# Second of seven projection products moved between the seventh and the third, fifth ahead of sixth, in blocks 2 to 5 of an attention and SwiGLU kernel

## The chip, the core and the metric

The kernel runs on one core of a Trainium2 chip. A core has five engines with their own instruction queues: TensorE (PE, matmuls; its weight loads are listed apart as PEld), VectorE (DVE), ScalarE (ACT), GpSimd (POOL) and SyncE (SP). An engine works through its queue in order and waits on semaphores for the others. The metric is the device time of one execution in microseconds (us); the figure for the kernel before is the median of nine runs.

## The reference

Two stages. Attention over 8 batches, 8 heads, 576 positions and head size 64, with a window of 128 positions and a bias that falls linearly with the distance; then a SwiGLU feed-forward over all 8 x 576 = 4608 tokens, model size 512, inner size 1536:

```python
scores = np.where(mask, scale * q @ k.T + bias, -1e9)   # mask: 0 <= i - j < 128
x = softmax(scores) @ v                                 # heads side by side: 4608 x 512
g = x @ w_gate
out = (g / (1 + exp(-g)) * (x @ w_val)) @ w_out         # float32
```

## The kernel before

**Blocks.** The feed-forward takes the tokens in nine blocks of 512 (`n` = 0 to 8). For a block, the gate and value products run over twelve slices `m` of the inner size: four 512-column matmuls into a PSUM tile `pg` for the gate, four into `pv` for the value. This text calls each of these groups of four a half step; a block has 24, numbered 0 to 23 (2 x `m` for the gate, 2 x `m` + 1 for the value). ACT makes `tt`, a tanh of the gate (L415), DVE makes `uu` from `tt` and `pg` (L416), and DVE multiplies `uu` by `pv` into `hT` (L427). `pg` and `pv` rotate through three PSUM banks.

**Attention** runs interleaved with blocks 0 to 5: scores (`ps`, L278, groups of eight matmuls; `psc`, L313), their exp on ACT (`ex`, L284; `exc`, L317), a multiply by decay factors or masks on DVE (L290, L321), weighted sums of values (`av`, L345), a division on DVE (L347, L348 into `x`), and a transpose of `x` on PE (`px`, L371) with an ACT copy, or by DMA on SP's queue. Scores, `av`, `px` and the tile `p2` described below share a pool of four PSUM banks, `ps_a`.

**The output projection by seven products.** The projection of block `n` - 1 is done during block `n`. Its tile of 512 tokens and its 512 output columns are each cut in two, the inner size is cut in two as well, and the 2 x 2 block product is made with seven products in place of eight (Strassen's scheme in Winograd's form). The function is `strassen(n, t)`; `t` is 0 or 1, each covers half of the rows of both token halves, so a block's projection is two runs of seven products, 14 in all. This text calls them the first half and the second half of the products of a block. A product is six 256-column matmuls (L532). Products are numbered as their helper names in the seven-product stage:

- first: `X` = A11 B11; ACT copies it out as `p1s`
- second: `p2` = A12 B21, in its own bank of `ps_a`; DVE adds `p1s` and makes the upper left quarter (profile name `osb<-p,p1s`)
- sixth: `X` += S2 T2; ACT copies it out as `u2s`
- fifth: `Y` = S1 T1; ACT copies it out as `p5s`
- seventh: `X` += S3 T3; DVE adds `p5s`, lower right quarter (`osb<-po,p5s`)
- third: `Y` += S4 B22; DVE adds `u2s`, upper right quarter (`osb<-po,u2s`), and SP stores the 128 rows
- fourth: `X` += A22 T4; ACT copies the lower left quarter out, and SP stores

`X` and `Y` are the two halves of one PSUM bank, the tile `po`, of which there is one. A product that writes there waits until the eviction of the product before it has read the bank. T1 to T4 are sums of parts of `w_out`, made once. S1 to S4 are sums of parts of `hT`, made on DVE by `sums(n, c)` in three thirds, c = 0, 1, 2, with four operations each (L485 to L488: S3, S1 in place of A21, S2, S4). They are queued in the list `later` from slice `m` = 9 on, and one or two are issued after each half step, so that the last third is issued during the first half steps of the next block. Third `c` is read by the matmuls 2c and 2c + 1 of a product's six.

**The order.** PE's order is the order of the program from step 60 on (`FIXED_FROM`), and blocks 2 to 5 lie there. In these blocks `AT` lists the half steps after which one product is issued; attention steps are issued by a count of the steps done so far. DVE's and ACT's order, the assignment of banks and the place of DMA instructions on SP are chosen by a scheduler when the program is built. POOL's queue is written out by hand. Blocks 6 to 8 have another scheme (`seven_steps`), in which gate and value products are also made by seven products; the projections of blocks 5 to 8 run there.

Of the kernel before, what the change touches and what calls it, by code (L numbers as in the profile page):

```python
# [51 lines left out]
def kernel(  # L52
# [10 lines left out]
    nc = tc.nc  # L63
    B, H, S, D = q.shape
    NTOK, DM = out.shape
# [370 lines left out]
    def rows_of(n, j):  # L436
        if n == 8:
            return [(0, 64, 2 * j * S + 512), (64, 128, (2 * j + 1) * S + 512)]
        return [(0, 128, n * S + j * P)]

    def store(n, j, osb, c0=0, c1=512, two=False):
        for i, (p0, p1, r0) in enumerate(rows_of(n, j)):
            (nc.scalar if two and i else nc.sync).dma_start(out[r0:r0 + p1 - p0, c0:c1],
                                                            osb[p0:p1, c0:c1])
# [18 lines left out]
    HC = DM // 2  # L463
    T1, T2, T3, T4 = (consts.tile([P, HM, HC], FP16, name=f"T{n}") for n in (1, 2, 3, 4))
    B11, B12 = wo_sb[:, 0:HM, 0:HC], wo_sb[:, 0:HM, HC:DM]
    B21, B22 = wo_sb[:, HM:NMB, 0:HC], wo_sb[:, HM:NMB, HC:DM]
# [37 lines left out]
    def strassen(n, t):  # L504

        h = hT[n]
        A11, A12 = h[:, 0:HM, 0:256], h[:, HM:NMB, 0:256]
        S1, A22 = h[:, 0:HM, 256:512], h[:, HM:NMB, 256:512]
        S2, S3, S4 = hsum[n]
        cols = slice(t * P, (t + 1) * P)  # L510
        end = n == NBLK - 1
        seeded = SEVEN_FROM <= n + 1 < NBLK
        factor = 1.0 if n >= SEVEN_FROM else 0.5
        if end:
            X, Y = (ps_a.tile([P, HC], FP32, name="po", tag="a", bufs=4) for _ in range(2))
            p2 = ps_f.tile([P, HC], FP32, name="p2", tag="gv")
        else:
            po = ps_f.tile([P, 2, HC], FP32, name="po", tag="po", bufs=1)
            X, Y = po[:, 0, :], po[:, 1, :]
            p2 = (ps_f.tile([P, HC], FP32, name="p2", tag="gv") if seeded  # L520
                  else ps_a.tile([P, HC], FP32, name="p2", tag="a"))
        top, low = (opool.tile([P, DM], FP32, name="osb", tag="osb") for _ in range(2))
        if end and t:
            spare = [opool.tile([P, DM], FP32, name="osb", tag="osb") for _ in range(2)]
            p1s, p5s, u2s = spare[0][:, 0:HC], spare[0][:, HC:DM], spare[1][:, 0:HC]
        else:
            p1s, p5s, u2s = (supool.tile([P, HC], FP32, name=i, tag=i, bufs=1)
                             for i in ("p1s", "p5s", "u2s"))

        def product(dst, a, b, start=False):  # L530
            for m in range(HM):
                nc.tensor.matmul(dst, a[:, m, cols], b[:, m, :], start=(start and m == 0),  # L532
                                 stop=(m == HM - 1), skip_group_check=True)

        def half_plus(dst, a, b):
            nc.vector.scalar_tensor_tensor(out=dst, in0=a, scalar=factor, in1=b,
                                           op0=ALU.mult, op1=ALU.add)

        product(X, A11, B11, True)
        if seeded:  # L540
            nc.scalar.copy(p2, X)
        else:
            nc.scalar.mul(p1s, X, factor)
        yield
        product(p2, A12, B21, not seeded)
        if seeded:
            nc.vector.tensor_scalar_mul(top[:, 0:HC], p2, factor)
        else:
            half_plus(top[:, 0:HC], p2, p1s)
        if end and t:  # L550
            store(n, t, top, 0, HC)
        yield
        product(X, S2, T2)
        nc.scalar.mul(u2s, X, factor)
        yield
        product(Y, S1, T1, end)
        if end and t:
            nc.vector.tensor_scalar_mul(p5s, Y, factor)
        else:
            nc.scalar.mul(p5s, Y, factor)  # L560
        yield
        product(X, S3, T3)
        half_plus(low[:, HC:DM], X, p5s)
        if end and t:
            store(n, t + 2, low, HC, DM, True)
        yield
        product(Y, S4, B22)
        half_plus(top[:, HC:DM], Y, u2s)
        store(n, t, top, HC if end and t else 0, DM, end)
        yield  # L570
        product(X, A22, T4)
        if end:
            nc.vector.tensor_scalar_mul(low[:, 0:HC], X, factor)
        else:
            nc.scalar.mul(low[:, 0:HC], X, factor)
        store(n, t + 2, low, 0, HC if end and t else DM, end)
        yield
# [118 lines left out]
                    of[which[0]][name](which[1])  # L696
                yield n, 7 * u + k, name, which

    AT = {1, 3, 4, 6, 8, 9, 11, 12, 14, 16, 17, 19, 20, 22}

    def ffn():

        for n in range(NBLK):
            if n > 1:
                parts = chain(strassen(n - 1, 0), strassen(n - 1, 1))
# [6 lines left out]
            for m in range(NMB):  # L712
                for half, _ in enumerate(gate_val(n, m)):
                    yield 1.0
                    if n > 1 and 2 * m + half in AT:
                        next(parts)
# [21 lines left out]
            if n > 1:  # L738
                assert next(parts, 0) == 0
        ends = [strassen(NBLK - 1, t) for t in range(2)]  # L740
        final = ()
        for n, k, name, which in seven_steps():
            if k == 0 and n > SEVEN_FROM:
                assert next(parts, 0) == 0
                parts = chain(strassen(n - 1, 0), strassen(n - 1, 1))
            if n == SEVEN_FROM and k in (1, 3, 10, 17):
                later.extend(gate_val_weight_sums(2 + (k + 4) // 7))
            yield 0.5
            if k % 3 == 2 and k < 42:
                next(parts)  # L750
                yield 0.75
            if k == 20 and n + 1 < NBLK:
                later.extend(x_sums(n + 1))
            if k == 35:
                later.extend(sums(n, 0))
            if name == "fourth" and which is not None and which[1] > 3:
                if which == (NBLK - 1, 5):
                    at_once(final)
                else:
                    later.extend(sums(which[0], which[1] - 3))  # L760
            if n == NBLK - 1 and k == 40:
                final = sums(n, 2)
                later.append(final.pop(0))
            for _ in range(2 if len(later) > 4 or k >= 39 or k < 7 else 1):
                if later:
                    later.pop(0)()
            if n == NBLK - 1 and k == 41:
                next(ends[0])
                yield 0.75
# [235 lines left out]
```

## Time and profile before

| | |
|---|---|
| median of nine runs | 345.09 us (344.87 to 345.57) |
| the profiled execution | 345.07 us, of which the span from first to last instruction is 343.3 us |
| PE busy | 329.1 us, 96% of the span |
| DVE busy | 277.6 us, 81% |
| ACT busy | 207.6 us, 60% |
| TensorE clock granted | 0.999 of full speed |
| the chain that ended last | PE 69%, DVE 19%, ACT 4%, DMA 4%, issue 3% of the span |
| first product of blocks 2, 3, 4, 5 starts at | 97.3, 136.2, 174.7, 212.5 us |
| seven-product stage starts at | 245.2 us |

Busy time is the sum of an engine's instruction records. PE's matmuls overlap, so the record of six 256-column matmuls is 0.82 us long while the next group starts 0.65 us after it; for times on PE the distance between starts is the better measure. DVE's and ACT's records overlap a little as well. A wait is put down to the engine and the line that released it.

### The profile page before, as it was taken

Reading aid. Unit: us, or ns where it says so; the run is one execution under the profiler, and the core shown is the slowest. Engines: PE = TensorE matmul, PEld = TensorE weight load, DVE = VectorE, ACT = ScalarE, POOL = GpSimd, SP = SyncE. Lnnn points to the kernel's source line nnn. Section 1 sums busy time; section 2 is a strip of 40 time slices with the busy share of each in tenths; the row PEclk is TensorE's granted clock in tenths of the full one; section 3 lists DMA queues with packets and bytes.
Section 4 is the critical chain, followed back from the end, with each engine's and each line's share of the span. In section 5 each row is a group of like instructions: output and inputs, shape, how many; then the busy total and the mean of one; then the engine's idle time right before and its main releaser. Section 6 shows DMA issues by size and latency. Waiting matters only on the chain.

```text
span 343.3 us, 7778 instructions
## 1 busy us (share of the span) xinstructions
PE 329.1 (96%) x2983; PEld 218.3 (64%) x2983; DVE 277.6 (81%) x652; ACT 207.6 (60%) x412; POOL 109.6 (32%) x136
## 2 busy tenths in 40 slices
PE   7999989999999999999999999999999999999995
PEld 3484455444456565666565655565788878888884
DVE  6578886999798679988899999999855975775683
ACT  3758676565666755756556557563467666676640
POOL 8968672649765076834017000000000000000000
PEclk9999999999999999999999999999999999999999
DMA  9999999999999999999939914021101101011014
GB/s 150 168 180 177 164 175 146 91 147 160 139 172 149 149 178 160 162 165 151 186 107 107 173 32 78 15 73 37 63 2 61 63 0 64 13 51 63 0 71 116
DMA packets 160037, 37.37 MB, mean 109 GB/s; under 512 B 147328, under 2 KB 155648, under 8 KB 160000
## 3 DMA queue, kind: packets, MB, share of 16 engines
q0 software_dynamic: 118336, 18.62, 84.1%
q1 hardware_dynamic: 40976, 17.64, 27.7%
q10 hardware_dynamic: 688, 0.62, 0.6%
q8 instruction: 23, 0.38, 0.5%
q14 instruction: 14, 0.11, 0.1%
HBM read 37.91 MB, written 9.44 MB: 138 GB/s over the span
## 4 chain that ended last, share of the span: by engine, by line
PE 69%; DVE 19%; ACT 4%; DMA 4%; issue 3%; POOL 0%; ACTq 0%; DVEq 0%
PE po L532 15%; PE pv L397 13%; PE pg L397 13%; PE gX L623 8%; PE gY L623 4%; PE av L345 3%; PE ps L278 3%; DVE uu L416 3%; DMA qn<-in_q_dram 3%; DVE hT L427 2%; PE p L532 2%; PE po L451 2%; PE gZ L623 2%; DVE x L348 2%; ACT ex L284 2%
## 5 line engine op out<-in xcount | busy, mean ns | idle before, releaser
L397 PE MATMUL pv<-xT,wv_sb 128*128 128x512 f16 (+2 forms) x320 | 76.5, 358 | 0.4 <-DVE hT L427 0.2
L397 PE MATMUL pg<-xT,wg_sb 128*128 128x512 f16 (+2 forms) x320 | 75.8, 358 | 0.3 <-DVE xT L373 0.2
L415 ACT ACTIVATE tt<-pg 128x512 f16<-128x512 f32 (+2 forms) x70 | 41.3, 590 | 50.4 <-PE pg L397 49.4
L284 ACT ACTIVATE ex<-ps 128x512 f16<-128x512 f32 x96 | 50.0, 606 | 11.3 <-PE ps L278 11.3
L416 DVE SCALAR_TENSOR_TENSOR uu<-tt,pg 128x512 f16<-128x512 f16 (+2 forms) x69 | 46.0, 666 | 10.4 <-ACT tt L415 10.2
L427 DVE TENSOR_TENSOR hT<-uu,pv 128x512 f16<-128x512 f16 (+2 forms) x70 | 46.7, 666 | 3.6 <-PE pv L397 1.6
L185 POOL DMA_DIRECT2D va<-in_v_dram x40 | 34.3, 865 | 38.3 <-PE av L345 31.9
L397 PEld LDWEIGHTS <-wg_sb 128*128 128x128 f16 x320 | 28.3, 98 | 24.1 <-issue 2.3
L532 PEld LDWEIGHTS <-hT 128*128 128x128 f16 x384 | 36.8, 98 | 10.4 <-issue 1.1
L397 PEld LDWEIGHTS <-wv_sb 128*128 128x128 f16 x320 | 28.3, 98 | 23.7 <-issue 2.6
L191 POOL DMA_DIRECT2D kn<-in_k_dram x39 | 33.3, 859 | 18.7 <-DMA kT<-kn 10.1
L191 POOL DMA_DIRECT2D qn<-in_q_dram x39 | 33.4, 863 | 16.1 <-DMA va<-in_v_dram 8.5
L532 PEld LDWEIGHTS <-S 128*128 128x128 f16 x288 | 27.7, 98 | 10.7 <-issue 2.5
L290 DVE TENSOR_TENSOR ex<-ex,m_reg 128x1024 f16<-128x1024 f16 x42 | 28.7, 687 | 3.2 <-ACT ex L284 3.1
L348 DVE TENSOR_TENSOR x<-av,rec 128x256 f16<-128x256 f32 x72 | 28.5, 419 | 0.4
L532 PE MATMUL po<-T,S 128*128 128x256 f16 x192 | 26.5, 273 | 0.5 <-DVE S L487 0.5
L532 PE MATMUL po<-T,hT 128*128 128x256 f16 x192 | 26.1, 273 | 0.0
L317 ACT ACTIVATE exc<-psc 128x512 f16<-128x512 f32 x40 | 21.3, 608 | 4.1 <-PE psc L313 4.1
L675 DVE TENSOR_TENSOR hT<-s,v 128x512 f16<-128x512 f16 x18 | 7.6, 424 | 18.5 <-ACT s L674 18.5
L345 PEld LDWEIGHTS <-ex 128*128 128x128 f16 x384 | 17.4, 97 | 4.6 <-issue 1.1
L345 PE MATMUL av<-va,ex 128*128 128x65 f16 x384 | 19.3, 194 | 0.7 <-ACT ex L284 0.7
L278 PE MATMUL ps<-qT,kT 64*128 64x256 f16 x192 | 16.6, 273 | 0.4 <-DVE qT L223 0.2
(134 smaller groups left out, 535.9 us busy)
## 6 DMA issues: line engine op xcount, KB each, us to landing
out_dram<-osb SPq DMA_DIRECT2D x32, 256.0 KB, 2.5
va<-in_v_dram POOLq DMA_DIRECT2D x32, 128.0 KB, 8.2
qn<-in_q_dram POOLq DMA_DIRECT2D x31, 128.0 KB, 8.7
kn<-in_k_dram POOLq DMA_DIRECT2D x31, 128.0 KB, 9.2
wg_sb<-in_moe_w_gate_dram POOLq DMA_DIRECT2D x6, 256.0 KB, 7.5
wv_sb<-in_moe_w_val_dram POOLq DMA_DIRECT2D x6, 256.0 KB, 8.0
wo_sb<-in_moe_w_out_dram POOLq DMA_DIRECT2D x2, 768.0 KB, 9.5
kn<-in_k_dram POOLq DMA_DIRECT2D x8, 64.0 KB, 7.0
```

The costliest lines, as they stand in the source:

```text
L185: nc.gpsimd.dma_start(va[rank][p0:p1, :, 0:D], src)
L191: nc.gpsimd.dma_start(t_[p0:p1], src)
L284: nc.scalar.activation(e[:, o:o + 2, :], banks[q4][par], AF.Exp, scale=scale)
L290: nc.vector.tensor_mul(e[:, o, :], e[:, o, :], reg[:, o, :])
L345: nc.tensor.matmul(av[:, j, :], w, val, start=(n == 0), stop=(n == len(todo) - 1))
L348: nc.vector.tensor_mul(x[:, 4 * half:4 * half + 4, :], av[:, :, 0:D], rec.broadcast_to([P, 4, D]))
L397: nc.tensor.matmul(ps[:, c0:c1], w[:, kb, ms], xT[n][:, kb, c0:c1], start=(kb == 0 and c0 == 0), stop=(kb == NKB - 1 and c1 == 512), skip_ ...
L415: nc.scalar.activation(tt, pg[:, c0:c1], AF.Tanh, scale=0.5)
L416: nc.vector.scalar_tensor_tensor(out=uu, in0=tt, scalar=one if (n, m) == PIN else 1.0, in1=pg[:, c0:c1], op0=ALU.add, op1=ALU.mult)
L427: nc.vector.tensor_mul(hT[n][:, m, c0:c1], acted[(n, m)][1][:, c0:c1], pv[:, c0:c1])
L532: nc.tensor.matmul(dst, a[:, m, cols], b[:, m, :], start=(start and m == 0), stop=(m == HM - 1), skip_group_check=True)
L623: nc.tensor.matmul(dst[:, i, :], w[:, kb, c0 + i * P:c0 + (i + 1) * P], a[:, kb, :], start=(start and i == 0 and kb == 0), stop=(i == 1 an ...
```

## The change

In `strassen` the steps become small functions, and their order depends on the block. Where the projection is that of blocks 1 to 4 (so in the blocks 2 to 5 of gate and value work) the order first, second, sixth, fifth, seventh, third, fourth becomes first, fifth, sixth, seventh, second, third, fourth. For the projections of blocks 5 to 8 it stays. `AT` gets other half steps for the 14 products:

| | first half of the products | second half |
|---|---|---|
| before | first 1, second 3, sixth 4, fifth 6, seventh 8, third 9, fourth 11 | first 12, second 14, sixth 16, fifth 17, seventh 19, third 20, fourth 22 |
| after | first 1, fifth 3, sixth 5, seventh 7, second 8, third 9, fourth 11 | first 13, fifth 15, sixth 17, seventh 19, second 20, third 21, fourth 23 |

The diff, with the bodies of the small functions left out; they hold the lines of before, unchanged:

```diff
-        product(X, A11, B11, True)
...
-        product(p2, A12, B21, not seeded)
...
-        product(X, S2, T2)
...
-        product(Y, S1, T1, end)
...
-        product(X, S3, T3)
...
-        product(Y, S4, B22)
...
+        def first():
+            product(X, A11, B11, True)
...
+        def second():
+            product(p2, A12, B21, not seeded)
...
+        def sixth():
+            product(X, S2, T2)
+            nc.scalar.mul(u2s, X, factor)
...
+        def fifth():
+            product(Y, S1, T1, end)
...
+        def seventh():
+            product(X, S3, T3)
+            half_plus(low[:, HC:DM], X, p5s)
...
+        def third():
+            product(Y, S4, B22)
+            half_plus(top[:, HC:DM], Y, u2s)
...
+        for step in ((first, second, sixth, fifth, seventh, third) if seeded or end
+                     else (first, fifth, sixth, seventh, second, third)):
+            step()
+            yield
         product(X, A22, T4)
...
-    AT = {1, 3, 4, 6, 8, 9, 11, 12, 14, 16, 17, 19, 20, 22}
+    AT = {1, 3, 5, 7, 8, 9, 11, 13, 15, 17, 19, 20, 21, 23}
```

In the built program PE, DVE, ACT and POOL have the same instructions as before. The order changes on PE, DVE and ACT from block 2 on, two transposes on SP change places with a store each, and POOL's order is the same.

More of the change, by code (lines that the diff above doesn't have):

```diff
@@ L537, in half_plus @@
                                            op0=ALU.mult, op1=ALU.add)
-        product(X, A11, B11, True)
[L540 to L544, printed above, removed]
-        product(p2, A12, B21, not seeded)
[L546 to L552, printed above, removed]
@@ L553, in strassen @@
-        product(X, S2, T2)
-        nc.scalar.mul(u2s, X, factor)
-        yield
-        product(Y, S1, T1, end)
[L557 to L561, printed above, removed]
-        product(X, S3, T3)
[L563 to L566, printed above, removed]
-        product(Y, S4, B22)
-        half_plus(top[:, HC:DM], Y, u2s)
-        store(n, t, top, HC if end and t else 0, DM, end)
@@ L570, in strassen @@
-        yield
+        def first():
+            product(X, A11, B11, True)
+            if seeded:
+                nc.scalar.copy(p2, X)
+            else:
+                nc.scalar.mul(p1s, X, factor)
+        def second():
+            product(p2, A12, B21, not seeded)
+            if seeded:
+                nc.vector.tensor_scalar_mul(top[:, 0:HC], p2, factor)
+            else:
+                half_plus(top[:, 0:HC], p2, p1s)
+            if end and t:
+                store(n, t, top, 0, HC)
@@ new lines, in sixth @@
+        def sixth():
[3 more added lines that the diff above has]
+            product(Y, S1, T1, end)
+            if end and t:
+                nc.vector.tensor_scalar_mul(p5s, Y, factor)
+            else:
+                nc.scalar.mul(p5s, Y, factor)
+        def seventh():
+            product(X, S3, T3)
+            half_plus(low[:, HC:DM], X, p5s)
+            if end and t:
+                store(n, t + 2, low, HC, DM, True)
+        def third():
+            product(Y, S4, B22)
+            half_plus(top[:, HC:DM], Y, u2s)
+            store(n, t, top, HC if end and t else 0, DM, end)
```

## The prediction

> **What bounds the kernel now.** I read the page's busy shares first, then PE's waits in the stretch where blocks 2 to 5 run (95 to 247 us), then four stages, then single places of the timeline. Columns of the page's first part are busy us, share of the span, instructions.
>
> ```profile
> PE 329.1 (96%) x2983; PEld 218.3 (64%) x2983; DVE 277.6 (81%) x652; ACT 207.6 (60%) x412; POOL 109.6 (32%) x136
> ```
>
> PE is the bound, so time can only be won where PE stands still. The waits of PE in the stretch (total, times, longest):
>
> ```profile
> PE po L532 <- DVE osb L536: 1.5, 2, 0.8
> PE p L532 <- ACT ex L284: 0.7, 1, 0.7
> PE av L345 <- ACT ex L284: 0.7, 2, 0.5
> PE po L532 <- DVE S L487: 0.5, 1, 0.5
> PE psc L313 <- DVE osb L536: 0.2, 1, 0.2
> ```
>
> All but the third are in steps that the change moves. The stages (length, then PE, PEld, DVE, ACT, POOL busy, granted clock, DMA):
>
> ```profile
> 95.00:165.00 70.00, 69.08 (x653) 42.22 (x653) 59.69 (x136) 45.41 (x92) 35.12 (x42) 1.00 1.97 161
> 165.00:194.00 29.00, 27.53 (x247) 16.73 (x246) 28.87 (x73) 15.70 (x33) 7.59 (x10) 1.00 1.44 136
> 194.00:245.00 51.00, 50.33 (x435) 30.11 (x434) 49.84 (x123) 26.89 (x53) 0.00 (x0) 1.00 0.24 58
> ```
>
> From 165 to 194 DVE works 28.87 of 29.00 us. There PE does not wait because its products are in a bad order; it waits because DVE is full, and a wait taken away at one place can come back at the next. The places, in PE's and DVE's timeline (start, length, instruction, idle before it):
>
> ```profile
> 118.06 0.61 PE L278 MATMUL ps<-qT,kT 64*128 64x256 f16 x8
> 119.36 0.82 PE L532 MATMUL p<-wo_sb,hT 128*128 128x256 f16 x6 [0.69 <-ACT ex L284]
> 139.23 0.82 PE L532 MATMUL p<-wo_sb,hT 128*128 128x256 f16 x6
> 140.17 0.42 DVE L486 TENSOR_TENSOR hT<-hT 128x512 f16<-128x512 f16 x1
> 166.91 0.39 PE L371 MATMUL px<-idm,x 128*128 128x128 f16 x4
> 167.92 0.81 PE L532 MATMUL po<-wo_sb,S 128*128 128x256 f16 x6 [0.63 <-DVE osb L536]
> 187.26 0.61 PE L278 MATMUL ps<-qT,kT 64*128 64x256 f16 x8
> 188.72 0.82 PE L532 MATMUL po<-wo_sb,S 128*128 128x256 f16 x6 [0.84 <-DVE osb L536]
> 216.90 0.60 PE L532 MATMUL po<-T,S 128*128 128x256 f16 x4
> 218.02 0.39 PE L532 MATMUL po<-T,S 128*128 128x256 f16 x2 [0.52 <-DVE S L487]
> 218.95 0.38 PE L313 MATMUL psc<-qT,kT 64*128 64x128 f16 x7 [0.15 <-DVE osb L536]
> ```
>
> Undisturbed, start to start, a half step (four 512-column matmuls) takes 0.86, a product (six 256-column ones) 0.65, eight score matmuls 0.54, a px 0.22. So the stalls cost: 119.36 (second waits for its bank, still read by an exp) 1.30 - 0.54 = 0.76; 167.92 (third waits for seventh's eviction) 1.01 - 0.22 = 0.79; 188.72 (the same) 1.46 - 0.54 = 0.92; block 5, sixth waits for S2 and the scores after it for second's bank, 1.45 - 0.65 and 0.91 - 0.55 = 1.16. A small one is in front of third at 129.21: the half step there takes 1.06, so 0.20. Together 3.83 us, all that can be won. In DVE's timeline a 512-column operation follows the last after 0.60, a 256-column one after 0.33.
>
> **What is removed, added, moved.** Nothing is removed or added: per block 14 products, 14 evictions (8 on ACT, 6 on DVE) and the stores stay. SP's stores follow third and fourth as before; two transposes on SP change places by one store, and POOL's queue is the same in the built order. I cost these at nothing: the loads they serve are needed several us later, and none of PE's waits above is for a DMA. First moving from half step 12 to 13 and fourth from 22 to 23 move PE work by one 0.86 half step against other PE work: nothing. The waits for ACT's evictions (p1s ahead of fifth, p5s ahead of sixth, u2s ahead of seventh) have two half steps, 1.7 us, against an eviction of 0.38 with at most one tanh of 0.60 ahead: covered; if ACT were three exps late (1.5 us) each would cost up to 0.4.
>
> Three things do move time; their operands and waits are read from the built order of the changed kernel.
>
> *1. Seventh to third.* Third now has second and another half step in front of it, 1.5 us more. The 0.20, 0.79 and 0.92 in front of third go at those places, and the 0.76 in front of second at 119.36 as well: second stands 2.7 us after the scores there.
>
> *2. Fifth at half step 3 needs S1.* DVE makes S1's last third (L486) at the start of each block; the last two of fifth's six matmuls need it. Before, half step 3 was second, which needs no sum. In block 3 that slot begins at 139.23. With 0.96 less stall before it (0.76 + 0.20) it begins at 138.27 and its fifth matmul wants S1 at 138.27 + 4 x 0.11 = 138.71. The operation ended at 140.17 + 0.42 = 140.59. In the changed order one eviction (osb<-p,p1s of block 2's second half, at 120.44 before, where DVE idled) falls into DVE's full stretch ahead of it: +0.33. The stretch begins earlier by the 0.76 and by the 0.65 of second, which no longer precedes the half step that opens it: -1.4. So S1 is there at 139.52, PE waits 0.8 and ends the product at 139.74, against 139.89 before: PE is 0.15 ahead, and no more. In block 4 L486 ended at 177.66; with another p1s eviction ahead (+0.33), an L290 multiply in place of a 256-column sum (+0.27) and the 0.15 it is there at 178.1. The slot was at 178.44: 178.44 - 0.79 - 0.15 + 0.35 (from 3) + 0.44 = 178.3, no wait. In block 5 the built order has S1 ahead of an L290 multiply (0.60) that preceded it: no wait; the 1.16 there go, because S2 has one half step more.
>
> *3. Second's bank.* Its result lies in one of the four ps_a banks that the scores rotate through, until DVE has done osb<-p,p1s. Before, 1.5 to 3 us lay between second and the next scores. Now in blocks 3 to 5 the scores follow 0 to 1.1 us after second, and either their last bank waits for that eviction (block 3 twice, block 4 first half), or the scores go round in the three other banks and wait for their own first exp (block 4 second half, block 5 first half). Block 3: 0 in the first half, where DVE has idle time; in the second the eviction stands behind a p5s eviction, an x and a uu from 166.9 and ends at 168.5, while PE asks at 168.2: about 0.35. Block 4, first half: DVE is full since 165.38, and up to this eviction it does what it did up to the end of osb<-po,p5s at 188.67, plus the p1s eviction of block 3's second half, which was at 159.57 in front of an idle time of 0.66: 188.67 + 0.33 - 0.15 = 188.85. PE asks for the bank at 187.8 - 0.79 - 0.15 + 0.35 - 0.2 = 187.0, so it waits 1.85; three score matmuls are left (0.2), and third starts at 189.05 against 188.72: **0.33 behind**. Everything won in 1 before this point is gone, because both orders meet DVE's queue here. The other two: the bank is free when four or eight score matmuls, their 0.17 of latency and one 0.61 exp are through, about 0.75 late each. The nearest row is the 0.76 at 119.36, with a tanh partly ahead. Ends: 0.3 if the records stretch the exp, 1.35 with a whole tanh of 0.60 ahead; I take 0.75.
>
> From block 4 on: 0.33 - 1.16 + 2 x 0.75 = **+0.67**. The profiled execution took 345.07 (span 343.3, 1.8 around it), 0.02 under the median of 345.09, so 345.07 + 0.67 = 345.7.
>
> A rule weighed: in the windows the clock stays 1.00 over PE idle times of up to 0.84 us, so my sum has no price for the clock. The Trainium skill, "TensorE: Matmul & The Clock Gate", Part 1, says that an idle window of about 3.4 us halves the clock; that speaks against a change that gathers waits into a longer one. By that rule as well my longest wait, 1.85, costs nothing more; if a wait filled such a window, an estimate from the page's figure adds 1.7 us, 347.4. No row here shows such a case.
>
> **The rivals.**
> - *The bank costs more (slower).* Place: the scores right behind second in block 4's second half and block 5's first. If ACT has a tanh (0.60) ahead of the exp that frees the bank, each costs 1.35 instead of 0.75: +1.2, 346.9. It decides once PE's half step ends less than 0.6 us before the exp can start. For it: second takes only 0.65 between that half step and the scores, and tt has waited behind exps elsewhere. Against it: ACT is busy 26.89 of 51.00 there.
> - *S1 in time.* If DVE opens its stretch 0.8 earlier than I think, block 3 keeps 0.96; then third in block 4 starts at 188.67 + 0.33 - 0.96 + 0.2 = 188.24, 0.48 ahead, and the sum is 0.48 + 1.16 - 1.5 = 0.14 faster: 344.9.
> - *Neither S1 nor the p1s eviction bites (faster).* Then all 3.83 go and only the two exp waits stay: 345.07 - 3.83 + 1.5 = 342.7. It needs DVE to do in less time what fills it from 165 to 194; against it speaks 28.87 of 29.00.
> - *No change.* The gaps are DVE's, and whatever PE wins is given back exactly: 345.1.
>
> **How the numbers follow.** A measurement of this kernel can tell about 0.2%, 0.69 us, from no change: faster is below 344.4, slower above 345.8. My forecast (345.0 to 346.6 by the ends of 2 and 3) has 0.42: 0.16 of it same, 0.26 slower, since most of its unknowns only add. The dearer bank has 0.22, slower. S1 in time 0.14: 0.05 faster, 0.09 same. Neither bites: 0.13, faster. No change: 0.09, same. Faster 0.18, same 0.34, slower 0.48. The range reaches from 344.0 to 347.3: it leaves out the case at 342.7 and 0.07 above.
>
> **What would show it.** Right: no "po L532 <- DVE osb L536" of 0.8 in front of third at the places above; in block 3 a wait of fifth for L486 of about 0.8; in the first half of block 4 scores that wait 1.5 to 2 us for osb<-p,p1s; twice about 0.7 of scores waiting for ACT in the second half of block 4 and in block 5; block 5's wait for S2 gone; the seven-product stage (245 to 338 before) later by 0.7 at its start and equally long. Wrong: PE's waits for DVE under 1 us in all between 130 and 230 (then faster), or waits of ACT-freed banks over 1 us each (then slower).

## The result, and the profile after

The changed kernel takes 346.57 us (median of 9 runs, 346.00 to 347.05); beside it the kernel before takes 345.04 (29 runs). The ratio is 1.004, with a 95% interval from 1.0032 to 1.0049: slower by 1.1 to 1.7 us. The profiled execution took 346.65 us, its span is 344.9 us. The line numbers behind `strassen` are 10 higher than before.

The page's first part (busy us, share of the span, instructions) shows the same instructions on every engine in a span longer by 1.6 us. PE's records have grown by 2.1 us, but 1.1 of that lies before block 2, and a group that stops for a wait leaves two records that are longer together (0.60 and 0.39 below, against 0.82 in one piece). So the busy time doesn't tell what the change cost; the starts do.

```profile
PE 331.2 (96%) x2983; PEld 219.0 (64%) x2983; DVE 277.0 (80%) x652; ACT 208.1 (60%) x412; POOL 109.6 (32%) x136
```

PE's waits in the same stretch as before, 95 to 247 us (waiting line, releaser, total us, times, longest):

```profile
PE ps L278 <- DVE osb L536: 0.6, 1, 0.6
PE psc L313 <- ACT exc L317: 0.6, 1, 0.6
PE po L532 <- DVE hT L486: 0.6, 1, 0.6
PE ps L278 <- ACT ex L284: 0.6, 1, 0.6
PE av L345 <- DMA kn<-in_k_dram: 0.5, 1, 0.5
PE pv L397 <- DVE uu L416: 0.3, 1, 0.3
PE ps L278 <- DVE x L348: 0.3, 1, 0.3
PE av L345 <- ACT ex L284: 0.2, 1, 0.2
```

Nothing of before's list is left but the `av` waits at about 95 us, ahead of everything that was changed (0.7 in both). No product waits in front of third any more. In their place stand the scores, waiting for the banks, the fifth product, waiting for S1 (L486), and a value half step, waiting for `uu`.

The stages (length, then PE, PEld, DVE, ACT, POOL busy, clock, DMA share, GB/s):

```profile
95.00:165.00 70.00, 68.74 (x645) 41.64 (x646) 59.66 (x135) 45.82 (x93) 36.80 (x44) 1.00 2.06 157
165.00:194.00 29.00, 28.00 (x253) 16.75 (x250) 29.00 (x73) 15.69 (x32) 7.59 (x10) 1.00 1.50 160
194.00:245.00 51.00, 49.45 (x431) 29.74 (x429) 48.22 (x120) 26.37 (x52) 0.00 (x0) 1.00 0.18 49
```

DVE is busy in all of the middle stage, 29.00 of 29.00, as it nearly was before. The granted clock is 1.00 in all three stages, as it was before, so no loss lies there. The places, in PE's timeline (start, length, instruction, idle before it and its releaser):

```profile
138.68 0.60 PE L532 MATMUL po<-T,hT 128*128 128x256 f16 x4
139.89 0.39 PE L532 MATMUL po<-T,hT 128*128 128x256 f16 x2 [0.61 <-DVE hT L486]
...
185.43 0.82 PE L532 MATMUL p<-wo_sb,hT 128*128 128x256 f16 x6
...
187.19 0.49 PE L278 MATMUL ps<-qT,kT 64*128 64x256 f16 x4
188.03 0.28 PE L278 MATMUL ps<-qT,kT 64*128 64x256 f16 x1 [0.34 <-DVE x L348]
188.96 0.38 PE L278 MATMUL ps<-qT,kT 64*128 64x256 f16 x3 [0.65 <-DVE osb L536]
189.26 0.83 PE L532 MATMUL po<-wo_sb,S 128*128 128x256 f16 x6
...
205.99 0.50 PE L278 MATMUL ps<-qT,kT 64*128 64x256 f16 x5
207.06 0.38 PE L278 MATMUL ps<-qT,kT 64*128 64x256 f16 x3 [0.58 <-ACT ex L284]
...
224.96 0.45 PE L313 MATMUL psc<-qT,kT 64*128 64x128 f16 x9
226.03 0.38 PE L313 MATMUL psc<-qT,kT 64*128 64x128 f16 x7 [0.63 <-ACT exc L317]
...
231.60 0.89 PE L345 MATMUL av<-va,exc 128*128 128x65 f16 x24
232.84 1.02 PE L397 MATMUL pv<-xT,wv_sb 128*128 128x512 f16 x4 [0.35 <-DVE uu L416]
```

The same places in DVE's timeline:

```profile
130.06 0.42 DVE L536 SCALAR_TENSOR_TENSOR osb<-p,p1s 128x256 f32<-128x256 f32 x1
130.39 0.42 DVE L485 TENSOR_TENSOR S<-hT 128x512 f16<-128x512 f16 x1
...
139.41 0.42 DVE L486 TENSOR_TENSOR hT<-hT 128x512 f16<-128x512 f16 x1
...
188.49 0.42 DVE L536 SCALAR_TENSOR_TENSOR osb<-p,p1s 128x256 f32<-128x256 f32 x1
...
232.11 0.68 DVE L416 SCALAR_TENSOR_TENSOR uu<-tt,pg 128x512 f16<-128x512 f16 x1
```

Each of the last three ends 0.05 or 0.06 us before the start of the PE instruction that it releases. The product at 138.68 goes on with its fifth matmul once the operation at 139.41 is done. The scores at 188.03 first wait for an `x`, then for second's bank, which the eviction at 188.49 frees 3.5 us after second began.

**The balance.** I measure the stretch from the first product of block 2 to the first of the seven-product stage, on PE's starts: 97.33 to 245.24 before, 147.91 us; 97.80 to 246.92 after, 149.12 us. That is **+1.21**. Block 2 begins 0.47 later in this execution, ahead of everything that was changed (the experiments begin there at 97.3 to 97.8, with either order), and the stage behind is as long as it was (98.06 and 97.98). Excess over the undisturbed period of each group:

| stall on PE, us | predicted | measured |
|---|---|---|
| the stalls of before (3.83, and 0.09 at 110.3) | gone | gone |
| block 3, fifth waits for S1 | 0.80 | 0.79 |
| block 3, scores, first half / second half | 0 / 0.35 | 0.23 / 0.22 |
| block 4 first half, second and the scores | 1.85 | 0.16 + 1.53 |
| block 4 second half, scores wait for their exp | 0.75 | 0.84 |
| block 5 first half, the same | 0.75 | 0.84 |
| block 5, value half step waits for `uu` | not seen | 0.51 |
| sum | 4.50 | 5.12 |

The "undisturbed" period depends a little on which group follows (a product ahead of `psc` takes 0.76 in place of 0.65), so a sum of this kind is good to about 0.1. Within that, 5.12 less 3.92, 1.20, accounts for the 1.21.

### The profile page after: what moved, and what is told of

It reads as the page before. It is cut to its first block, busy times and chain, and to the rows that moved or that the text cites. A ratio compares the mean times of both kernels' runs of the same rounds, so it can differ in the third digit from the quotient of the medians.

```text
span 344.9 us, 7773 instructions
## 1 busy us (share of the span) xinstructions
PE 331.2 (96%) x2983; PEld 219.0 (64%) x2983; DVE 277.0 (80%) x652; ACT 208.1 (60%) x412; POOL 109.6 (32%) x136
## 4 chain that ended last, share of the span: by engine, by line
PE 76%; DVE 15%; ACT 5%; issue 2%; DVEq 0%
PE po L532 16%; PE pg L397 14%; PE pv L397 14%; PE gX L633 8%; PE gY L633 4%; PE av L345 4%; PE ps L278 4%; PE po L451 2%; PE p L532 2%; DVE uu L416 2%; PE gZ L633 2%; DVE hT L427 2%; PE px L371 2%; ACT ex L284 2%; PE psc L313 1%
## 5 line engine op out<-in xcount | busy, mean ns | idle before, releaser
L278 PE MATMUL ps<-qT,kT 64*128 64x256 f16 x192 | 17.5, 273 | 2.0 <-DVE osb L536 0.6
```

The lines of the kernel that those rows point to most:

```text
L278: nc.tensor.matmul(two[par][:, j, :], kT[rows, ks, pair, :], qT[rows, p:p + 2, pair, :], start=(j == 0 and not early_tile), stop=(j == 1))
```

## Experiments

Each was timed in five rounds beside the kernel before; "stretch" is the length defined above, less before's 147.91, from one profiled execution. Theory A is the prediction's: PE's own work is unchanged, and the new order pays for what it removes by waiting for S1 and for second's bank, both of which hang on DVE's queue. Its main rival holds that DVE's total work decides, so that nothing moved on PE can matter. A further one, formed after the first runs, is that the S1 wait hangs on the half step of seventh, the last reader of S3. Every edit is a new build, in which the scheduler chooses DVE's and ACT's order anew, so a run differs from its neighbour by more than the line shown.

### The two halves of the change

*Only the half steps (old order):*

```diff
-    AT = {1, 3, 4, 6, 8, 9, 11, 12, 14, 16, 17, 19, 20, 22}
+    AT = {1, 3, 5, 7, 8, 9, 11, 13, 15, 17, 19, 20, 21, 23}
```

> The old order of the products with the new half steps. Theory A (the new order costs, through S1 and through the bank of second): second stays at half step 3, far from the next scores, fifth no longer needs S1 early; the waits of third for seventh's eviction stay (0.2 + 0.8 + 0.9), the wait of sixth for S2 in block 5 (0.80) goes: 344.2 to 345.2 us. Theory B (the later half steps of first and fourth cost): 345.8 to 346.6.

Measured: 344.32 us, ratio 0.9974 (0.996 to 0.9988), stretch -0.75. The time is inside the range, but not by the places that were expected. The 0.76 in front of second in block 2 is gone, and neither an S1 wait nor a wait for S2 is left. Four stalls are left: 0.54 and 1.02 in front of third, 0.39 for a `uu`, and 1.19 in block 5, where the `psc` scores that begin at 217.08 stop 0.98 for second's eviction. So second's bank, thought free in the old order, costs there too.

*Only the order (old half steps):* the changed kernel with

```diff
-    AT = {1, 3, 5, 7, 8, 9, 11, 13, 15, 17, 19, 20, 21, 23}
+    AT = {1, 3, 4, 6, 8, 9, 11, 12, 14, 16, 17, 19, 20, 22}
```

> The new order of the products with the old half steps. Theory A: fifth still stands at half step 3 (a wait of about 0.8 for S1 in block 3) and second still right ahead of scores, so 346.0 to 347.0 us. Theory B: about 345.0, as before.

Measured: 344.75 us, ratio 1.000 (0.9982 to 1.0018), stretch -0.45. **This missed.** Theory A had the S1 wait come from the order, but with the old half steps it is not there. In PE's timeline of this kernel:

```profile
138.23 0.82 PE L532 MATMUL po<-T,hT 128*128 128x256 f16 x6
...
185.78 0.50 PE L278 MATMUL ps<-qT,kT 64*128 64x256 f16 x5
187.73 0.38 PE L278 MATMUL ps<-qT,kT 64*128 64x256 f16 x3 [1.46 <-DVE osb L536]
```

Fifth runs its six matmuls in one piece. The wait for second's bank in block 4 is there in full, 1.72 as a stall. So neither half of the change is slow by itself; together they are. Fifth early needs S1 early, and here it comes early: its last third ends at 137.62, against 139.83 in the changed kernel. The old half steps put the second half's seventh at 17 once the order is new; the new ones leave it at 19, where the kernel before has it. In the kernel before S1 ended at 140.59, and nothing waited, because fifth came later.

### The S1 wait

*Fifth one half step later:* the changed kernel with

```diff
-    AT = {1, 3, 5, 7, 8, 9, 11, 13, 15, 17, 19, 20, 21, 23}
+    AT = {1, 4, 5, 7, 8, 9, 11, 13, 15, 17, 19, 20, 21, 23}
```

> The changed kernel with fifth at half step 4 in the first half of the products. Theory A1 (S1's wait of 0.79 in block 3 is a cost of its own): the wait goes and most of it is kept, 345.6 to 346.0 us. Theory A2 (DVE is full, so what PE wins in block 3 is waited for in block 4): the wait for the p1s eviction in front of third in block 4 grows from 1.5 to about 2 and the total stays at 346.3 to 346.7.

Measured: 345.85 us, ratio 1.0022 (1.0012 to 1.0032), stretch +0.68. The S1 wait is gone; a wait of 0.47 of scores in block 3 came. The form of theory A by which block 4 gives all of it back is wrong: the bank wait there stayed at 1.53 and did not grow, and the eviction that it waits for came 0.87 earlier by the trace (0.52 without the earlier start of block 2): DVE's full stretch moves forward together with PE.

*Seventh of the second half from half step 19 to 17, what lies before it closer:* the changed kernel with

```diff
-    AT = {1, 3, 5, 7, 8, 9, 11, 13, 15, 17, 19, 20, 21, 23}
+    AT = {1, 3, 5, 7, 8, 9, 11, 13, 15, 16, 17, 20, 21, 23}
```

Why this place: the tile of S3 exists once. Its last reader is seventh of the second half, and L485, the first of the sums, writes it anew for the next block, so the series of sums can't begin before seventh. (The edit also moves sixth, the last reader of S2, from 17 to 16.)

> The changed kernel with, in the second half of the products, sixth at 16 and seventh at 17 in place of 17 and 19. S2 to S4 have one buffer each, and seventh is the last reader of S3, which DVE writes first among the next block's sums. Theory D (seventh at 19 holds the next sums back into the stretch where DVE is full): DVE starts them up to 2 us earlier, in idle time; fifth's wait for S1 in block 3 (0.79) goes and the wait in front of third in block 4 (1.5) shrinks: 344.8 to 345.8 us. Theory A (the order itself puts fifth too early): the wait for S1 stays, 346.3 to 346.8.

Measured: 345.01 us, ratio 0.9993 (0.9985 to 1.0002), stretch -0.14. In DVE's timeline of this kernel:

```profile
124.24 0.42 DVE L536 SCALAR_TENSOR_TENSOR osb<-po,p5s 128x256 f32<-128x256 f32 x1 [0.19 <-PE po L532]
124.58 0.75 DVE L485 TENSOR_TENSOR S<-hT 128x512 f16<-128x512 f16 x2
125.25 0.42 DVE L486 TENSOR_TENSOR hT<-hT 128x512 f16<-128x512 f16 x1
...
137.15 0.42 DVE L486 TENSOR_TENSOR hT<-hT 128x512 f16<-128x512 f16 x1
```

The sums start at 124.58, right behind seventh's eviction; in the changed kernel seventh's eviction comes at 127.73 and the first of the sums at 130.39, in DVE's full stretch, after DVE had idled for 1.06 and 0.29 us between 124.5 and 126.5. The last L486 then comes at 137.15 in place of 139.41. S1's 0.79 and the 0.51 for `uu` in block 5 are gone, 1.30 of the 1.35 won. The bank wait in block 4, which was expected to shrink, is there as before (1.53), and so are both exp waits. So in this order an earlier seventh is enough to remove the S1 wait, and the `uu` wait with it. That a late seventh alone makes S1 late is not so: with only the half steps changed seventh stands at 20, and S1's last third ends at 138.75, 1.1 us before the changed kernel's (0.7 without the different starts of block 2). There the eviction of second, at 130.06 in the changed kernel, does not stand ahead of the sums.

### Second's bank

*ACT empties second's bank, DVE adds later from SBUF:* the changed kernel with

```diff
-                half_plus(top[:, 0:HC], p2, p1s)
+                nc.scalar.copy(top[:, 0:HC], p2)
+                half_plus(top[:, 0:HC], top[:, 0:HC], p1s)
```

> The changed kernel with second's result copied out of its bank by ACT into the output tile, and p1s added there by DVE afterwards: the bank no longer waits for DVE's queue; DVE has as many operations as before, ACT eight more for each block. Theory A (the bank is what costs in block 4): the 1.5 us in front of third in block 4 fall below 0.5, the two waits for an exp (0.84 each) stay or shrink: 344.8 to 345.7 us. Theory C (DVE is full, PE waits at the next place): 346.3 to 346.8.

Measured: 344.01 us, ratio 0.9968 (0.9959 to 0.9977), stretch -1.10, more than was expected. (ACT gets two copies more per block, ten in all, not eight per block.) PE's timeline in block 4's first half, then ACT's:

```profile
186.61 0.50 PE L278 MATMUL ps<-qT,kT 64*128 64x256 f16 x5
187.44 0.39 PE L278 MATMUL ps<-qT,kT 64*128 64x256 f16 x3 [0.33 <-DVE x L348]
```

```profile
185.67 0.37 ACT L551 COPY osb<-p 128x256 f32<-128x256 f32 x1
```

The bank is free at 186.04, before the scores begin; DVE's add still runs at 187.90, late as ever, and nobody waits for it. What is left there is the wait for `x`, which the changed kernel has as well: of its 1.53 second's bank makes 0.92. The stall falls to 0.61, not below 0.5 as expected, and those of the exp waits from 0.84 to 0.29 each; that the scores find the fourth bank free fits this, but no run separates it. S1 still costs 0.77. Ten copies cost ACT 3.7 us, in time that it has.

*The same on the kernel before* (old order, old half steps):

> The kernel before with second's bank copied out by ACT and nothing else. There second stands far from the next scores, and only the 0.36 in block 5 is a wait for its bank: 344.5 to 345.2 us. If ACT's eviction wins for another reason than the bank's place in the new order: 343.5 to 344.2.

Measured: 344.73 us, ratio 0.999 (0.9981 to 0.9998), stretch -0.34. With second far from the next scores there is little to win: of the listed stalls only a bank wait of 0.36 goes.

### How much of it is DVE's load

*No weight sums, with the kernel before and with the changed one:*

```diff
-        return [lambda: nc.vector.tensor_sub(t1, V1[:, :, cols], G1[:, :, cols]),
...
+        return []
```

> The kernel before without the 24 sums of the gate and value weights (L597 to L600, 0.33 us each on DVE, most of them between 176 and 238 us); their tiles are read as they are. Theory C (DVE's load makes PE wait): the waits of third in block 4 (0.92) and in block 5 (1.16) go: 342.6 to 343.4 us. Theory A alone (places of waits, not load): 344.5 to 345.1.

> The changed kernel without the same 24 sums. Theory C: the wait in front of third in block 4 (1.7 with the second product's) and the one for uu in block 5 (0.5) go, the wait for S1 in block 3 (0.79) and the two for an exp (0.84 each) stay: 344.0 to 344.8 us, so still 1 to 2 us above the kernel before made light in the same way. If DVE's load is the whole cause, both light kernels are within 0.5 us of each other.

Measured: 344.25 us, ratio 0.9972 (0.9963 to 0.998), stretch -0.88, for the kernel before without them; 344.98 us, ratio 0.9995 (0.9984 to 1.0006), stretch -0.27, for the changed one. Both kernels compute the last blocks from whatever the tiles of the sums hold, so only their times count. **Both missed.** For the kernel before the time lies between the two theories: the 0.92 in block 4 goes, as theory C has it, but the 1.16 in block 5 stays. The changed kernel lies just above its range, and 0.73 above the light kernel before, in place of 1 to 2. So 24 operations less on DVE halve the difference between the two orders, from 1.53 to 0.73 by the medians and from 1.21 to 0.61 by the stretch; the noise leaves open whether the medians differ by less than the 0.5 named. The waits tell more: in the changed kernel the block 4 wait falls from 1.53 to 0.67 and the wait for `uu` goes, but S1 (0.77) and the two exp waits (0.84 each) stay. DVE's load sets the size of the first two; the others are there without it. That nothing moved on PE could matter is ruled out by the runs above that keep all of DVE's operations: by the order of products and the half steps alone they reach from 344.32 us (only the half steps) to 346.57.

### Another order, and the parts together

*The old order with seventh a half step earlier, so that a half step lies between it and third (in the first half sixth moves one later as well):* the kernel before with

```diff
-    AT = {1, 3, 4, 6, 8, 9, 11, 12, 14, 16, 17, 19, 20, 22}
+    AT = {1, 3, 5, 6, 7, 9, 11, 12, 14, 16, 17, 18, 20, 22}
```

> The old order with sixth at 5, fifth at 6, seventh at 7 and third at 9, in the second half of the products seventh at 18 and third at 20: third is two half steps from seventh and second stays where it was. Theory A: the waits of third (0.2 + 0.8 + 0.9) and of sixth for S2 (0.8) go, the bank of second costs nothing new; some of it comes back as other waits for DVE: 343.0 to 344.5 us. Theory C (DVE is full, every wait taken away comes back): 345.0.

Measured: 344.05 us, ratio 0.9972 (0.9962 to 0.9983), stretch -1.06. In PE's waits, third's for seventh's eviction fall from 1.5 to 0.2, with 0.3 for the eviction of p5s and 0.4 of `psc` new; second's 0.76 stays. So most of third's waiting for seventh goes without moving second. (The profiled execution of this kernel started 3.7 us late, so it is read from block 2 on alone.) With ACT emptying second's bank:

> The old order with third two half steps behind seventh, second's bank copied out by ACT. Without ACT's copy its remaining waits were 0.76 in front of second, 0.65 of the scores in block 5 for the bank, and 0.3 to 0.4 three times. The 0.65 goes: 343.3 to 343.9 us. If it moves elsewhere: 344.0 to 344.3.

Measured: 343.66 us, ratio 0.9957 (0.9945 to 0.9969), stretch -1.31. The 0.65 falls to 0.38, there a wait for an `x`.

*Seventh at 17, and ACT for second's bank:*

> Both cures of the changed kernel together: sixth at 16 and seventh at 17 in the second half of the products, and second's bank copied out by ACT. If the wait for S1 (0.77) and the waits for the bank are causes of their own, both savings add up: 344.0 less 0.8 to 1.2, so 342.7 to 343.4 us. If DVE's load returns one of them: 343.8 to 344.4.

Measured: 342.88 us, ratio 0.9944 (0.9928 to 0.996), stretch -2.36. Against the changed kernel the two edits alone won 1.35 and 2.31, 3.66 together; both at once won 3.57 of stretch. By the medians it is 4.1 and 3.7. So they are two causes, nearly separate, and together three times the loss.

*The new order with the old half steps, and ACT for second's bank:*

> The new order with the old half steps, second's bank copied out by ACT. The order alone still waited 1.7 in front of third in block 4 and 0.85 and 0.4 behind second in blocks 5 and 4; if these are the bank, they fall to about 0.6, 0.3 and 0: 342.4 to 343.4 us, the fastest of all. If not: 344.3 to 344.9.

Measured: 342.33 us, ratio 0.9923 (0.991 to 0.9936), stretch -2.48. It has the lowest median, 2.8 us under the kernel before, which ran at 345.10 beside it; it lies just under its range, and by the intervals it can't be told from the run before this one. All that the view of PE's waits still lists from 95 to 247:

```profile
PE av L345 <- ACT ex L284: 0.7, 2, 0.5
PE po L532 <- DVE osb L536: 0.3, 1, 0.3
```

Its scores in block 4's first half, where the changed kernel loses 1.53, run in one piece directly behind second and a half step, in PE's timeline:

```profile
184.19 0.82 PE L532 MATMUL p<-wo_sb,hT 128*128 128x256 f16 x6
185.00 1.02 PE L397 MATMUL pv<-xT,wv_sb 128*128 128x512 f16 x4
185.96 0.65 PE L278 MATMUL ps<-qT,kT 64*128 64x256 f16 x8
```

## Why the prediction was right, and where it was off

**Right.** The time lies inside the range and on the side that had the largest chance, and it got there by the steps that were forecast.

- *Seventh to third* (step 1): the waits of third for seventh's eviction and second's 0.76 are gone at all four places.
- *Fifth needs S1* (step 2): the product at 138.68 has its fifth matmul start at 139.89 with a stall of 0.79, for which 0.8 was worked out from DVE's queue; the wait came only in block 3. The eviction of second stands ahead of the sums, at 130.06, as said, and with 0.47 taken off for the later start S1 is there at 139.36, against 139.52. The work behind the product is 0.24 ahead of before, against 0.15 predicted.
- *Second's bank, block 4* (step 3): the three last score matmuls at 188.96 follow the eviction at 188.49, as said, and DVE's stage is full. Not seen was the `x` that holds the scores at 188.03 first: without second's bank 0.61 of the 1.53 would still be there.
- The seven-product stage came 1.21 later, without the different start of block 2, where 0.7 was said, and was equally long.
- No price for the clock: it is 1.00 in the stage that holds the longest stall, 1.53.

**Off in size.** The sum was +0.67, the stretch shows +1.21. Up to third in block 4 the estimate was too dear: 0.33 behind was predicted, 0.07 is measured (189.26 less 0.47, against 188.72). Second and the scores lost 1.69 there in place of 1.85. From there to the end of the stretch +0.34 was predicted and +1.14 came. Three terms make the difference of 0.80:

- *The two exp waits*, 0.84 each, not 0.75: +0.18. ACT's timeline shows no queue ahead of them. The tanh ends at 206.04, and the exp starts at 206.41, 0.42 after the scores at 205.99. PE goes on at 207.06, 0.65 after the exp's start. So 1.07 go by before the sixth matmul, and 0.31 for the last three make 1.38, for a group that takes 0.54 undisturbed.
- *The wait for `uu` in block 5*: +0.51. It was not in the sum at all. I followed the operands of the products that were moved, but not the half step behind them: its bank is freed by `uu`, and this stood in DVE's queue behind an `x` and three weight sums (231.10 to 232.11). The term that was missing belongs to the sum "From block 4 on", which has nothing for DVE's queue in block 5. Without the weight sums the wait is gone, and with the sums early it is gone too.
- 0.11 over several small places.

ACT's timeline at the first of the two exp waits:

```profile
205.44 0.60 ACT L415 ACTIVATE tt<-pg 128x512 f16<-128x512 f32 x1 [1.88 <-PE pg L397]
206.41 2.07 ACT L284 ACTIVATE ex<-ps 128x512 f16<-128x512 f32 x4 [0.38 <-PE ps L278]
```

Two readings in the prediction are off without changing the sum. Before, 2.3 to 4.1 us lay between second and the next scores in blocks 3 to 5, not 1.5 to 3. And the ends given for the exp waits, 0.3 and 1.35 each, span 344.8 to 346.9, wider than the 345.0 to 346.6 to which the forecast's chance was given.

The medians differ by 1.53, with an interval that reaches down to 1.1. The 0.3 between that and the stretch was not traced to a place; the start of block 2 moves by as much from one execution to another.

**The reasons behind the steps.** One of the prediction's causes is incomplete and one does not hold as put. The S1 wait was ascribed to fifth's new place and one more eviction on DVE. Both are in the trace, but the order alone has no such wait: with the old half steps the new order has seventh of the second half at 17, and the sums run in DVE's idle time from 124.58 on. The new half steps leave seventh at 19, as before, and the sums begin at 130.39 in DVE's full stretch. And the sentence that everything won before block 4 is gone "because both orders meet DVE's queue here" is wrong in general: seventh at 17 and fifth at 4 kept what they won ahead of it, since DVE's queue moves forward too. The rival "S1 in time" was priced at 344.9, and the kernel that brings S1 in time measured 345.01, stretch -0.14 as worked out. That the sums agree so well is luck: third in block 4 starts 0.77 ahead there and not 0.48, and dearer exp waits take most of the rest back.

The rival by which neither S1 nor the p1s eviction bites was priced at 342.7 and thought to need DVE to do its work in less time. The two kernels that remove both waits measured 342.88 and 342.33, without taking an operation from DVE.

## What to carry to other kernels

When a product moves, follow its PSUM bank to the bank's next user: who empties it, through which in-order queue, and what stands ahead in that queue. If the emptying engine is full there, let an engine with slack copy the bank out and do the arithmetic later from SBUF. Follow as well the last reader of every tile that exists once, because its place decides when the producer of the next block may start. Here a producer that missed the idle time ran in the busy one.

## What the runs showed of the hardware

DVE's scaled add of 128x256 float32 took as long with its first operand in SBUF as with it in PSUM. The groups of instructions (line, operation, tile, shapes, count, busy us, mean ns, idle before), first of the changed kernel, then of the one with ACT's copy:

```profile
L536 DVE SCALAR_TENSOR_TENSOR osb<-p,p1s 128x256 f32<-128x256 f32 x9 | 3.7, 416 | 0.0
```

```profile
L536 DVE SCALAR_TENSOR_TENSOR osb<-osb,p1s 128x256 f32<-128x256 f32 x9 | 3.7, 416 | 0.0
```

It is 416 ns both times, so the add itself gains nothing by the move. What is gained is the earlier release of the bank, and the price is ACT's 372 ns per copy.
